# A convolution feeding a gated feed-forward layer on one core: the opening's taps, casts, bands and loads rearranged

## The chip, the core and the metric

The kernel runs on one core of a Trainium2 chip. The metric is device time in microseconds (us), the median of several runs. Engines are named as in the profile: PE is TensorE (PEld its weight loads), DVE is VectorE, ACT is ScalarE, POOL is GpSimd, SP is SyncE, which here only issues transfers. A "q" behind a name (SPq) is the engine's instruction queue.

## The reference

A causal convolution of seven taps along the sequence, with softmax-normalised taps per head, and then a feed-forward layer with the gate h * cos(h):

```python
w = exp(weight - max(weight))          # weight: 8 heads x 7 taps
w = w / (sum(w) + 1e-9)
x_pad = concatenate([zeros(B, 6, D), x], axis=1)
x_unf = x_pad[:, idx, :].reshape(B, S, 7, 8, 24)
y = einsum('hk,bskhg->bshg', w, x_unf).reshape(32768, 192)
h = y @ w_in                            # 192 -> 2048
out = (h * cos(h)) @ w_out              # 2048 -> 192
```

B is 8, S 4096, D 192; everything comes and goes in float32.

## The kernel before

**Main loop.** The 32768 tokens are 64 tiles of 512 (index t), two tiles to a unit of 1024 (index u). For each tile, PE makes eight groups h0 to h7 of the hidden layer (`mm1`, L503, into three PSUM buffers `h`), ACT takes the cosine (L510), DVE multiplies (L514), and PE forms the output in 64 steps of `mm2` (L552). The order of PE's and ACT's work is written out by hand in strings: `PE_FIRST` and `ACT_FIRST` for the first tiles, `PE_ORDER` and `ACT_ORDER` for the rest. "m12" is twelve steps of mm2, "h3" an mm1 group, "s3" its cosine and product, "w5" five zero products, "r", "d" and "c" are parts of the convolution of coming units, "K" casts, "L" loads, "X", "Y", "T" transposes and edges, "W" the cast of half of w_out; "p" marks that a tile's 64 steps are through, so that P and Q (copies of the output out of PSUM) may follow, and "q" is a check at half a tile.

**Opening.** Before the first mm1 the first half of unit 0 must be convolved on PE. The convolution is a product with a band matrix `band` (128 x 8 heads x 256, bf16), which is built from the taps:

- `w_row` (L81) brings the 8 x 7 weights into four partitions. `quarter` (L140 to L144), a 4 x 128 matrix with ones in a block of 32 columns for each row, is made on POOL by a memset and two selections. One fp32 product (L150) spreads the four rows over four blocks of 32 partitions.
- softmax: L176 to L185 on DVE, with the exponential on ACT (L179). `mask` (L158, L159 on POOL, then copied to the other three blocks at L164 by DVE and ACT) times the taps is `prod` (L401), its sum `diag` (L404).
- sixteen copies of 32 x 76 put the pieces of `diag` into `band` (L415). The string "DPDPDPDPDPDPDPAA" gives their engines in turn. Copies 0 to 3 complete heads 0 and 1, 4 to 7 heads 2 and 3, and so on.
- x of unit 0, first half, is loaded at the very start and cast to bf16 (`cast_unit`, L219) on ACT. Its other half and unit 1 are loaded behind a no-op on SP that waits for `diag`; the loads of w_out (`load_wo`, L124, four transfers) come behind a second no-op, after `conv_first`. w_in is loaded and cast by two transfers that POOL issues (`load_w`, L112).
- PE is kept busy meanwhile with products of zeros (`keep_warm`, L136): three before L150, nine after it.
- `conv_first` (L432, copied out at L438) and `turn_first` (L453, L457) make the first four blocks of transposed input `cT`; then the main loop begins. POOL casts the rest of unit 0 (L219), unit 1, and the two halves of w_out (`cast_wo`, L120), in that order of its queue.

Each engine works its own queue in order; waits between engines are set by the data that instructions share and by the no-ops named above.

Of the kernel before, what the change touches and what calls it, by code (L numbers as in the profile page):

```python
# [8 lines left out]
FP32 = mybir.dt.float32  # L9
BF16 = mybir.dt.bfloat16  # L10
AF = mybir.ActivationFunctionType
ALU = mybir.AluOpType
# [4 lines left out]
def kernel(  # L17
# [8 lines left out]
    nc = tc.nc  # L26
    B, S, D = x.shape
    H, K = weight.shape
# [3 lines left out]
    T = 512  # L32
    NT = NTOK // T
    NB = T // 128
    U = 1024
# [41 lines left out]


    HQ = H // 4
    w_row = consts.tile([4, HQ * K], FP32)  # L80
    nc.scalar.dma_start(out=w_row, in_=weight.rearrange("(q h) k -> q (h k)", q=4))  # L81

    x_tiles = {}

# [40 lines left out]

    one = consts.tile([128, 1], FP32)
    nc.vector.memset(one, 1.0)
    zero = consts.tile([128, T], BF16)  # L130
    nc.vector.memset(zero, 0.0)  # L131
# [2 lines left out]
    def keep_warm(n, bank=idle):  # L134
        for _ in range(n):
            nc.tensor.matmul(out=bank, lhsT=zero[:, 0:128], rhs=zero, start=True, stop=True)  # L136


    quarter = consts.tile([4, 128], FP32)
    nc.gpsimd.memset(quarter, 1.0)  # L140
    nc.gpsimd.affine_select(out=quarter, in_=quarter, compare_op=ALU.is_ge, fill=0.0, base=0, pattern=[[1, 128]],
                            channel_multiplier=-32)
    nc.gpsimd.affine_select(out=quarter, in_=quarter, compare_op=ALU.is_ge, fill=0.0, base=31, pattern=[[-1, 128]],
                            channel_multiplier=32)  # L144
    scrap = consts.tile([128, 1], FP32)
    nc.scalar.activation(out=scrap, in_=one, func=AF.Exp)
    keep_warm(3)
    w_all = o_pools[1].tile([128, T], FP32, name="o_ps1")
    w_bc = w_all[:, 0 : HQ * K].rearrange("p (h k) -> p h k", k=K)
    nc.tensor.matmul(out=w_all[:, 0 : HQ * K], lhsT=quarter, rhs=w_row, start=True, stop=True)  # L150
    keep_warm(9)


    xb0 = consts.tile([128, UB + 1, D], BF16, name="x_bf0")
# [22 lines left out]
    wexp = consts.tile([128, HQ, K], FP32)  # L177
    nc.vector.tensor_tensor(out=wexp, in0=w_bc, in1=wmax.to_broadcast([128, HQ, K]), op=ALU.subtract)
    nc.scalar.activation(out=wexp, in_=wexp, func=AF.Exp)  # L179
    nc.scalar.activation(out=scrap, in_=one, func=AF.Sin)  # L180
    wsum = consts.tile([128, HQ, 1], FP32)
    nc.vector.tensor_reduce(out=wsum[:, :, 0], in_=wexp, axis=mybir.AxisListType.X, op=ALU.add)
    winv = consts.tile([128, HQ, 1], FP32)
# [168 lines left out]
    def taps(u, j, half, mul):  # L352
        if u not in pa:
            pa[u] = pa_pool.tile([128, PA, WN, OR], FP32, name="pa")
        part = slice(HALF * half, HALF * (half + 1))
        mul(pa[u][:, j, part], tap_window(u, j)[:, part], tap[:, j : j + 1])  # L356

# [1 line left out]

    def conv_raw(u):  # L360

        a, p = pa.pop(u), raw_prod
        nc.gpsimd.tensor_tensor(out=p, in0=tap_window(u, PA, K),  # L363
                                in1=tap[:, PA:K].rearrange("p (j a b) -> p j a b", a=1, b=1).to_broadcast([128, K - PA, WN, OR]),
                                op=ALU.mult)
        add = nc.gpsimd.tensor_tensor
        n, done = K - PA, 0
        while done < PA:
            m = min(n, PA - done)
            add(out=p[:, 0:m], in0=p[:, 0:m], in1=a[:, done : done + m], op=ALU.add)  # L370
            done += m
        while n > 2:
            m = n // 2
            add(out=p[:, 0:m], in0=p[:, 0:m], in1=p[:, n - m : n], op=ALU.add)  # L374
            n -= m
        ro[u] = ro_pool.tile([128, WN, OR], BF16, name="ro")
        add(out=ro[u], in0=p[:, 0], in1=p[:, 1], op=ALU.add)  # L377
# [17 lines left out]
                              in_=c[:, UB].rearrange("p c (n t) -> p n c t", t=16)[:, :, :, 8 : 8 + K - 1])  # L395


    cast_unit(0, 0, NB, nc.scalar.copy)

    prod = consts.tile([128, HQ, E, K], BF16)  # L400
    nc.vector.tensor_tensor(out=prod, in0=mask.rearrange("p (o e) k -> p o e k", o=1).to_broadcast([128, HQ, E, K]),  # L401
                            in1=wn.rearrange("p h (o k) -> p h o k", o=1).to_broadcast([128, HQ, E, K]), op=ALU.mult)
    diag = consts.tile([128, HQ, E], FP32)
    summed = nc.vector.tensor_reduce(out=diag, in_=prod, axis=mybir.AxisListType.X, op=ALU.add)  # L404

    tc.add_manual_dep(nc.sync.nop().ins, summed.ins.name, sync_dep, reason="order of the transfers")
    load_unit(0, NB, UB)
    load_unit(1, 0, NB)
    load_unit(1, NB, UB)
    load_edges(1)  # L410

    three = {"D": nc.vector.tensor_copy, "A": nc.scalar.copy, "P": nc.gpsimd.tensor_copy}
    for i, k in enumerate("DPDPDPDPDPDPDPAA"):
        q, rows = divmod(i, 4)
        three[k](out=band[32 * rows : 32 * rows + 32, HQ * q : HQ * (q + 1), 32 * rows : 32 * rows + E],  # L415
                     in_=diag[32 * q : 32 * q + 32])
    cast_unit(0, NB, UB)
    nc.gpsimd.memset(pick, 0.0)
    for i in range(2):
# [157 lines left out]
    def finish(t):  # L577
        o_sb[t] = opool.tile([128, NB, D], FP32, name="o_sb")
        for si in range(2):
            for b in range(2):  # L580
# [5 lines left out]

    PE_ORDER = ['m12 h0 m4 h1 K+3 R+1 m5 h2 m7 q h3 U+0 m6 h4 m17 h5 X+1 m9 p h6 h7 O m4', 'm11 h0 m4 h1 m6 h2 m7 q x+1 h3 m5 h4 m7 c1 m8 c2 m3 h5 T+3 L+4 m9 p O h6 h7 m4']
    ACT_ORDER = ['s0 s1 a211 s2 s3 s4 a014 a114 Q s5 P s6 s7 a007', 's0 s1 s2 a102 s3 a203 s4 Q ec2 ec1 s5 P s6 s7']  # L590

    PE_FIRST = ["K1 h0a h0b W0 h1 h2 h3 r h4 w5 d11 w4 h5 d21 W1 c11 X0 m1 h6 m11 h7 L2 c21 D1",
                "m6 K2 h0 m1 L3 h1 K3 m13 q h2 m3 h3 m9 h4 m6 h5 m3 X1 c12 m11 p c22 h6 d12 h7 L4 L5 m17 c13 m4 c23 m1 d22 Y1 D2 m1",
                "h0 m2 h1 m7 q K4 h2 m11 h3 X2 O m8 h4 Y2 m13 p h5 h6 m9 h7 m7",
                "h0 m8 h1 m8 q h2 m7 h3 m7 O m1 h4 m3 d13 m4 d23 m6 h5 m4 p T4 h6 h7 m4 D3 Z0 Z1",
                'm12 h0 m4 h1 K+3 m5 h2 m7 q h3 m6 h4 m17 h5 X+1 m9 p h6 h7 O m4',
                'm11 h0 m4 h1 m6 h2 m7 q x+1 Y3 h3 m5 h4 m7 c1 m8 c2 m3 h5 T+3 L+4 m9 p O h6 h7 m4']
    ACT_FIRST = ["s0a s0b s1 s2 er s3 s4 ed11 ed21 s5 ec11 s6 ec21 s7",
                "s0 s1 s2 s3 s4 s5 ec12 ec22 Q P s6 ed12 s7 ed22 ec13 ec23",
                "s0 s1 s2 s3 Q s4 P s5 s6 s7",  # L600
                "s0 s1 s2 s3 s4 ed13 ed23 Q s5 P s6 s7"] + ACT_ORDER

    PE_LAST = "m10 h0 m3 h1 m13 h2 m2 q h3 m10 h4 m3 h5 m7 h6 m12 p h7 O m7"
    ACT_LAST = "s0 s1 s2 s3 s4 s5 s6 P A s7"

    HALVES = {"": (0, NB), "a": (0, NB // 2), "b": (NB // 2, NB), "l": (0, NB // 2), "r": (NB // 2, NB)}
# [5 lines left out]
    for t in range(NT + 1):  # L612
        u, second = divmod(t, TPU)
        cu = u + TPU
        if t >= 2 * TPU:
            if second:
                conv["c"] = conv_unit(cu, ring_banks) if cu < NU else iter(())
        pe = PE_LAST if t == NT - 1 else "m%d p" % (2 * STEPS * NT - step) if t == NT else PE_ORDER[second] if t >= len(PE_FIRST) else PE_FIRST[t]
        act = ACT_LAST if t == NT - 1 else ACT_ORDER[second] if t >= len(ACT_FIRST) else ACT_FIRST[t]
        act, h = act.split(), {}  # L620
        done = {k for k in done if k[0] in "cd" and k[2:]}
# [4 lines left out]
        def flush():  # L626
            while act:
                k = act[0]
                if k[0] == "e":
                    need = k[1:] if k[1:] in conv else k[1] + "2" + k[3:]  # L630
                else:
                    need = "p" if k in "PQA" else "h" + k[3:] if k[0] in "ab" else "h" + (k[1:2] if k[2:] in "lr" else k[1:])
                if need not in done:
                    return
                act.pop(0)
                if k in "PQA":
                    if 0 <= made < NT - 1:
                        evac(made, int(k != "P"), nc.scalar.copy if k == "A" else None)
                elif k[0] in "ab":
                    if u + 2 in rT:  # L640
                        taps(u + 2, int(k[1]), int(k[2]), nc.scalar.mul if k[0] == "a" else nc.vector.tensor_scalar_mul)
                elif k[0] == "e":
                    next(conv[part_of(k[1:])], None)
                elif k[0] == "s" and t < NT:
                    gcu(t, int(k[1]), h[k[1:2] if k[2:] in "lr" else k[1:]], *HALVES[k[2:]])
# [17 lines left out]
        for k in pe.split():  # L663
            if k[0] == "h":
                if t < NT:
                    h[k[1:]] = mm1(t, int(k[1]), *HALVES[k[2:]])
            elif k[0] in "rdc":
                next(conv[part_of(k)], None)
            elif k[0] == "m":
                for q in range(step, step + int(k[1:])):  # L670
                    mm2_step(q)
                step += int(k[1:])
            elif k[0] == "w":
                keep_warm(int(k[1:]), o_pools[0].tile([128, T], FP32, name="o_ps0"))
            elif k == "p":
                assert step % (2 * STEPS) == 0
                made = step // (2 * STEPS) - 1
            elif k == "q":
                assert step % (2 * STEPS) == STEPS
            elif k[0] == "W":  # L680
                cast_wo(int(k[1]))
            elif k == "O":
                while stored <= made and (stored, 0) in evacs and (stored, 1) in evacs:
                    store(stored)
                    stored += 1
            elif k[1:] and k[1] != "+":
                of_unit(k[0], int(k[1]))
            else:
                if u + int(k[2:]) < NU and (k[0] not in "RUx" or u + int(k[2:]) >= FIRST_RAW):
                    of_unit(k[0], u + int(k[2:]))  # L690
            done.add(k)
            flush()
            if k == "p" and made == NT - 1:
                finish(NT - 1)
        assert t == NT or not act


# [28 lines left out]
```

## Time and profile before

| | us |
|---|---|
| median of 3 runs (lowest, highest) | 705.16 (705.04, 705.51) |
| the profiled execution | 705.18 |
| its span | 703.5 |
| PE busy | 697.0 (99% of the span) |
| DVE busy | 642.4 (91%) |
| ACT busy | 644.4 (92%) |
| POOL busy | 503.7 (72%) |
| mean granted clock of PE | 0.999 |

The profile follows one execution. "Busy" is the time in which an engine has an instruction running. A timeline line gives the start from the span's begin, the length, engine, source line, operation, the tile written and the tiles read, the shapes, how many instructions were merged, and in brackets the idle time before with what ended it. The chain is followed back from the last instruction through what released each step. In a table of stretches each engine has its busy time and, in parentheses, its instruction count; the last three columns are the granted clock, the share of the DMA engines and GB/s.

### The profile page before, as it was taken

The numbers are of one execution on the slowest core, as the hardware profiler recorded it, in microseconds if no ns is written. First come the engines' busy times: TensorE is split into PE (matmuls) and PEld (weight loads), VectorE is DVE, ScalarE is ACT, GpSimd is POOL, SyncE is SP. The second block draws the span as 40 slices with busy tenths as digits, with TensorE's granted clock in tenths as the row PEclk, the third lists the DMA queues.
The fourth block names the chain that finished last, engine by engine and source line by source line (L and its number), as shares of the span: only waits on it lengthen the run. The fifth ranks groups of instructions, "written<-read, shape, count | busy, mean of one in ns | idle before, by whom it ended". The sixth has DMA issues, their size and how long they took to land.

```text
span 703.5 us, 26826 instructions
## 1 busy us (share of the span) xinstructions
PE 697.0 (99%) x11830; PEld 512.8 (73%) x11830; DVE 642.4 (91%) x598; ACT 644.4 (92%) x831; POOL 503.7 (72%) x214
## 2 busy tenths in 40 slices
PE   8999999999999999999999999999999999999997
PEld 4677777777777777777777777777777777777776
DVE  6889999999999999999999999999999999999996
ACT  7889999999999999999999999999999999999875
POOL 6524478977778877778877688877789778799400
PEclk9999999999999999999999999999999999999999
DMA  8964456667667768676656577577665576874331
GB/s 214 234 167 97 120 135 143 138 147 164 138 153 146 131 145 176 134 152 131 147 152 153 150 159 129 140 161 150 143 147 132 145 174 137 153 127 95 92 91 47
DMA packets 228292, 100.09 MB, mean 142 GB/s; under 512 B 156240, under 2 KB 227792, under 8 KB 228176
## 3 DMA queue, kind: packets, MB, share of 16 engines
q1 hardware_dynamic: 227464, 97.40, 62.7%
q8 instruction: 92, 1.51, 0.9%
q0 software_dynamic: 416, 0.79, 0.7%
q14 instruction: 24, 0.20, 0.1%
q10 hardware_dynamic: 296, 0.20, 0.1%
HBM read 31.36 MB, written 25.17 MB: 80 GB/s over the span
## 4 chain that ended last, share of the span: by engine, by line
PE 96%; DMA 1%; DVE 1%; POOL 0%; SPq 0%; ACT 0%; issue 0%; POOLq 0%
PE o_ps L552 48%; PE h L503 46%; PE h L277 2%; DMA wo_f<-in_moe_w_out_dram 1%; PE h L552 0%; SPq L124 0%; PE h L229 0%; DVE band L415 0%; POOL wo L120 0%; POOL mask L159 0%; DVE ct L438 0%; PE o_ps L432 0%; ACT mask L164 0%; DVE diag L404 0%; DVE prod L401 0%
## 5 line engine op out<-in xcount | busy, mean ns | idle before, releaser
L514 DVE TENSOR_TENSOR g<-h,cs 128x1024 bf16<-128x1024 f32 (+1 forms) x513 | 604.9, 1216 | 27.9 <-ACT cs L510 24.5
L510 ACT ACTIVATE cs<-h 128x1024 bf16<-128x1024 f32 (+1 forms) x513 | 511.0, 1021 | 44.0 <-PE h L503 30.6
L552 PEld LDWEIGHTS <-g 64*128 64x128 bf16 x8192 | 354.2, 94 | 102.2 <-issue 1.0
L552 PE MATMUL o_ps<-wo,g 64*128 64x192 bf16 x8128 | 420.6, 243 | 0.1
L503 PE MATMUL h<-cT,w 64*128 64x512 bf16 (+1 forms) x3078 | 407.0, 376 | 0.8 <-DVE g L514 0.4
L503 PEld LDWEIGHTS <-w 64*128 64x128 bf16 x3078 | 147.6, 94 | 75.0 <-issue 1.8
L211 POOL CAST xk<-x_f 128x768 bf16<-128x768 f32 (+1 forms) x56 | 76.4, 1367 | 113.9 <-DMA x_f<-in_x_dram 109.3
L363 POOL TENSOR_TENSOR raw_prod<-rT,tap 128x2784 f32<-128x2784 bf16 x28 | 135.3, 4832 | 0.2
L370 POOL TENSOR_TENSOR raw_prod<-raw_prod,pa 128x2088 f32<-128x2088 f32 x28 | 129.1, 4609 | 2.2
L356 ACT ACTIVATE pa<-rT,tap 128x348 f32<-128x348 bf16 x168 | 94.6, 580 | 0.0
L374 POOL TENSOR_TENSOR raw_prod<-raw_prod 128x1392 f32<-128x1392 f32 x28 | 87.9, 3138 | 2.2
L571 DVE COPY o_sb<-o_ps 128x384 f32<-128x384 f32 x62 | 34.6, 557 | 23.7 <-PE o_ps L552 23.5
L377 POOL TENSOR_TENSOR ro<-raw_prod 128x696 bf16<-128x696 f32 x28 | 46.5, 1660 | 2.2
L294 ACT CAST ct_buf<-h 112x480 bf16<-112x480 f32 x56 | 28.6, 562 | 4.1 <-PE h L277 0.6
L571 ACT COPY o_sb<-o_ps 128x384 f32<-128x384 f32 x64 | 30.8, 482 | 0.1
L277 PE MATMUL h<-xk,band 64*112 64x120 bf16 x448 | 21.2, 213 | 0.0
L277 PEld LDWEIGHTS <-band 64*112 64x112 bf16 x448 | 18.0, 127 | 0.0
L219 POOL CAST x_bf<-x_f 128x768 bf16<-128x768 f32 (+2 forms) x5 | 9.1, 1812 | 7.0 <-DMA x_f<-in_x_dram 6.9
L307 POOL COPY ct<-ct 128x1728 bf16<-128x1728 bf16 x3 | 4.9, 1630 | 8.9 <-ACT ct L239 8.9
L394 POOL COPY cT<-cT 128x144 bf16<-128x144 bf16 x3 | 0.9, 308 | 13.5 <-DMA cT<-ct 13.5
L136 PE MATMUL o_ps<-zero 128*128 128x512 bf16 x21 | 7.2, 492 | 1.3 <-DVE zero L131 1.3
L239 ACT CAST ct<-h 128x432 bf16<-128x432 f32 x12 | 5.9, 530 | 0.4 <-issue 0.4
(66 smaller groups left out, 52.7 us busy)
## 6 DMA issues: line engine op xcount, KB each, us to landing
out_dram<-o_sb SPq DMA_DIRECT2D x63, 384.0 KB, 3.7
x_f<-in_x_dram SPq DMA_DIRECT2D x28, 480.0 KB, 5.5
x_f<-in_x_dram SPq DMA_DIRECT2D x56, 192.0 KB, 2.7
cT<-ro SPq DMA_DIRECT2D x112, 87.0 KB, 2.3
x_f<-in_x_dram SPq DMA_DIRECT2D x4, 384.0 KB, 5.6
wo_f<-in_moe_w_out_dram SPq DMA_DIRECT2D x4, 384.0 KB, 7.9
x_f<-in_x_dram SPq DMA_DIRECT2D x2, 768.0 KB, 5.2
cT<-ct_buf SPq DMA_TRANSPOSE x56, 4.0
```

The source lines that it names most:

```text
L211: copy(out=xk[u][:, NC * n0 : NC * n1].rearrange("p (k n) m -> p k n m", k=NC), in_=x_tiles[u][:, n0:n1].rearrange("p n (m k) -> p k n m", ...
L277: return nc.tensor.matmul(out=ps[h // 4][0:OP, 0 : NPB * 4 * G].rearrange("p (m i r) -> p i m r", m=NC * NPB, i=4)[:, h % 4], lhsT=band[si ...
L356: mul(pa[u][:, j, part], tap_window(u, j)[:, part], tap[:, j : j + 1])
L363: nc.gpsimd.tensor_tensor(out=p, in0=tap_window(u, PA, K), in1=tap[:, PA:K].rearrange("p (j a b) -> p j a b", a=1, b=1).to_broadcast([128, ...
L370: add(out=p[:, 0:m], in0=p[:, 0:m], in1=a[:, done : done + m], op=ALU.add)
L374: add(out=p[:, 0:m], in0=p[:, 0:m], in1=p[:, n - m : n], op=ALU.add)
L377: add(out=ro[u], in0=p[:, 0], in1=p[:, 1], op=ALU.add)
L503: nc.tensor.matmul(out=h[:, i, n0 * 128 : n1 * 128], lhsT=w[rows, k, j, :], rhs=rhs, start=(k == 0), stop=(k == NC - 1))
L510: nc.scalar.activation(out=cs[:, :, part], in_=h[:, :, part], func=AF.Sin, bias=math.pi / 2.0, scale=1.0)
L514: nc.vector.tensor_tensor(out=g_tiles[t][:, 2 * j : 2 * j + 2, part], in0=h[:, :, part], in1=cs[:, :, part], op=ALU.mult)
L552: ms.append(nc.tensor.matmul(out=o_ps[tt, b, si], lhsT=g_tiles[tt][rows, f, s * 128 : (s + 1) * 128], rhs=wo[rows, f // 2, f % 2, :], star ...
L571: (copy or copies[b])(o_sb[t][:, 2 * b : 2 * b + 2, :].rearrange("p s d -> p (s d)"), o_ps.pop((t, b)))
```

## The change

The weights go into one partition (`w_row` 1 x 4 x 14), `one` becomes 128 x 32, and four products of a 1 x 32 row of ones with 14 weights each replace the product with `quarter`, which goes. Eleven zeros follow instead of nine. x's first cast goes to POOL (the default of `cast_unit`). The band copies are dealt out as "DAPDAPDAPDAPDADA" and come before the SP no-op, which now waits for the last of them; the loads of unit 0's rest and unit 1 follow it. Further, in the part behind the opening, "p" and "q" leave the strings, and the "m" loop itself notes when a tile's 64 steps are complete; a few assertions are added; the tokens a and b may name a unit.

```diff
-    w_row = consts.tile([4, HQ * K], FP32)
-    nc.scalar.dma_start(out=w_row, in_=weight.rearrange("(q h) k -> q (h k)", q=4))
+    w_row = consts.tile([1, 4, HQ * K], FP32)
+    nc.scalar.dma_start(out=w_row, in_=weight.rearrange("(o q h) k -> o q (h k)", o=1, q=4))
...
-    one = consts.tile([128, 1], FP32)
+    one = consts.tile([128, 32], FP32)
...
-    quarter = consts.tile([4, 128], FP32)
-    nc.gpsimd.memset(quarter, 1.0)
-    nc.gpsimd.affine_select(out=quarter, in_=quarter, compare_op=ALU.is_ge, fill=0.0, base=0, pattern=[[1, 128]],
-                            channel_multiplier=-32)
-    nc.gpsimd.affine_select(out=quarter, in_=quarter, compare_op=ALU.is_ge, fill=0.0, base=31, pattern=[[-1, 128]],
-                            channel_multiplier=32)
...
-    nc.tensor.matmul(out=w_all[:, 0 : HQ * K], lhsT=quarter, rhs=w_row, start=True, stop=True)
-    keep_warm(9)
+    for q in range(4):
+        nc.tensor.matmul(out=w_all[32 * q : 32 * q + 32, 0 : HQ * K], lhsT=one[0:1], rhs=w_row[:, q], start=True, stop=True)
+    keep_warm(11)
...
-    cast_unit(0, 0, NB, nc.scalar.copy)
+    cast_unit(0, 0, NB)
...
-    summed = nc.vector.tensor_reduce(out=diag, in_=prod, axis=mybir.AxisListType.X, op=ALU.add)
-
-    tc.add_manual_dep(nc.sync.nop().ins, summed.ins.name, sync_dep, reason="order of the transfers")
+    nc.vector.tensor_reduce(out=diag, in_=prod, axis=mybir.AxisListType.X, op=ALU.add)
+
+    three = {"D": nc.vector.tensor_copy, "A": nc.scalar.copy, "P": nc.gpsimd.tensor_copy}
+    for i, k in enumerate("DAPDAPDAPDAPDADA"):
+        q, rows = divmod(i, 4)
+        m = three[k](out=band[32 * rows : 32 * rows + 32, HQ * q : HQ * (q + 1), 32 * rows : 32 * rows + E],
+                     in_=diag[32 * q : 32 * q + 32])
+    tc.add_manual_dep(nc.sync.nop().ins, m.ins.name, sync_dep, reason="order of the transfers")
     load_unit(0, NB, UB)
     load_unit(1, 0, NB)
     load_unit(1, NB, UB)
     load_edges(1)
-
-    three = {"D": nc.vector.tensor_copy, "A": nc.scalar.copy, "P": nc.gpsimd.tensor_copy}
-    for i, k in enumerate("DPDPDPDPDPDPDPAA"):
...
             elif k[0] == "m":
-                for q in range(step, step + int(k[1:])):
-                    mm2_step(q)
-                step += int(k[1:])
+                for _ in range(int(k[1:])):
+                    mm2_step(step)
+                    step += 1
+                    if step % (2 * STEPS) == 0:
+                        made = step // (2 * STEPS) - 1
+                        done.add("p")
+                        flush()
+                        if made == NT - 1:
+                            finish(NT - 1)
...
-            elif k == "p":
-                assert step % (2 * STEPS) == 0
-                made = step // (2 * STEPS) - 1
-            elif k == "q":
-                assert step % (2 * STEPS) == STEPS
```

## The prediction

> **What bounds the kernel.** I read the page's chain first, then the waits from 20 us to the end, then the first 24 us in order of time.
>
> ```profile
> span 703.5 us, 26826 instructions
> ...
> PE 96%; DMA 1%; DVE 1%; POOL 0%; SPq 0%; ACT 0%; issue 0%; POOLq 0%
> ```
>
> The chain in order of time (start, length) has, after 8.84 us of a w_out transfer:
>
> ```profile
> 21.00 0.02 issue
> 21.02 0.02 POOLq L120
> 21.04 0.08 issue
> 21.12 1.48 POOL wo L120
> 22.60 0.04 issue
> 22.64 0.34 PE o_ps L552 x4
> ```
>
> From 22.64 to 699.9 us TensorE never lets go of the chain: 677 us of its own work, which this diff leaves alone, and behind it only the last copy and store. What the change is worth is how far it moves that 22.64, so the opening is the only stage to cost. The page's 91 to 92% for VectorE and ScalarE play no part.
>
> Two roads lead to 22.64. Road A is computation: the softmax taps become the band, the first convolution runs, the first mm1 starts. Road B is transfers: w_out lands at 21.00 and is cast by L120.
>
> ```profile
> 2.06 0.96 POOL L159 TENSOR_SCALAR_AFFINE_SELECT mask<-mask 32x266 bf16<-32x266 bf16 x1
> 2.70 0.60 PE L150 MATMUL o_ps<-w_row,quarter 4*128 4x14 f32 x2
> 2.98 1.43 POOL L112 DMA_DIRECT2D w<-in_moe_w_in_dram  x2
> 3.55 0.17 DVE L178 TENSOR_TENSOR wexp<-o_ps,wmax 128x14 f32<-128x14 f32 x1
> 3.91 0.21 ACT L179 ACTIVATE wexp<-wexp 128x14 f32<-128x14 f32 x1
> 5.28 0.71 DVE L404 TENSOR_REDUCE diag<-prod 128x76 f32<-128x532 bf16 x1
> 6.02 1.86 DVE L415 CAST band<-diag 32x76 bf16<-32x76 f32 x7
> 6.13 2.00 POOL L415 CAST band<-diag 32x76 bf16<-32x76 f32 x7 [0.73 <-DVE diag L404]
> 10.60 1.62 PE L503 MATMUL h<-cT,w 64*128 64x256 bf16 x18 [0.18 <-DVE cT L457]
> 11.73 1.23 POOL L219 CAST x_bf<-x_f 128x768 bf16<-128x768 f32 x1 [3.59 <-DMA x_f<-in_x_dram]
> 22.05 0.93 PE L552 MATMUL o_ps<-wo,g 64*128 64x192 bf16 x12
> ```
>
> In this timeline the bands are the last thing before the convolution: GpSimd's seventh ends at 8.13, 2.14 after diag (5.99). Road A has a slack of about 0.27 at the end: of the twelve matmuls at 22.05, eight need only w_out's first half and at the usual 40 ns each are through near 22.37; the other four wait for 22.64.
>
> **The change, part by part.** Road A first.
>
> Taps. One fp32 product has two passes, 0.24 us apart (0.60 in all less 0.38, the longest one's length, rounded up). Four products make eight passes. No row shows a 128x32 fp32 weight. From above: the same 0.24 per pass; the taps then end 6 x 0.24 = 1.4 later. From below: L337's two small bf16 products (0.20 us in all, each some 0.17) are 0.03 apart, so eight passes end about as early as now. I take 0.10, nearer the low end since only a quarter of the columns is loaded: 7 x 0.10 less 0.24 = +0.46. Of this 0.16 is hidden: the exponential started at 3.91 although its input was ready at 3.72, because ScalarE was still copying the mask (L164, to 3.88). That copy comes earlier, since GpSimd loses the three quarter instructions (0.19 + 0.28 + 0.28 and their gaps, 0.85) and the mask is ready at 2.2. So diag: +0.30 (bounds -0.15 to +1.3). The Trainium skill, "TensorE: Matmul & The Clock Gate", section "LDWEIGHTS (loading the stationary operand)", makes the load's time proportional to columns; that would be an estimated 0.06 per pass and diag at about 0.0 instead of +0.30. No row here tests it.
>
> Bands. Sixteen copies go from 7 D, 7 P, 2 A to 6 D, 6 A, 4 P. At their rows: D 6 x 0.27 = 1.60; A 6 x 0.255 = 1.53; P 4 x 0.29 = 1.14. The longest, 1.60, replaces 2.14: -0.54. ScalarE is free in time: exponential, 1.28 of table load, 0.20, all before diag ends, as it no longer casts x.
>
> x cast by GpSimd. 1.23 for the same shape (11.73 row) instead of 1.21 on ScalarE. Behind two w issues, two memsets and ident, which end at 5.40 now and 4.55 then, it ends at 5.8, before diag at 6.3: costed at nothing. The first x load lands 3.4 after its issue at 0.82, so it doesn't wait. The cover is 0.5; beyond that every 0.1 delays the four P copies, which have another 0.46 before they are last. The row speaks of a cast beside a VectorE that reads PSUM; VectorE's band copies take 0.19 alone and 0.25 to 0.29 beside GpSimd's, so a mutual slowing of a third is the upper end: 6.2, still covered. The Trainium skill, "GPSIMD Engine Reference", section "Specifications", says that GpSimd shares its SBUF interface with VectorE when that has two SBUF inputs; by it prod (L401, 0.48) would stretch, at most by a third, and road A lose 0.15.
>
> Eleven zeros. The early ones are 0.43 apart, later ones 0.22; the step came at about 5.9.
>
> ```profile
> 5.34 0.15 PEld L136 LDWEIGHTS <-zero 128*128 128x128 bf16 x1 [0.28 <-issue]
> ...
> 5.77 0.15 PEld L136 LDWEIGHTS <-zero 128*128 128x128 bf16 x1 [0.28 <-issue]
> ...
> 6.12 0.10 PEld L136 LDWEIGHTS <-zero 128*128 128x128 bf16 x1 [0.20 <-issue]
> ```
>
> Starting at 3.6, six at 0.43 reach 6.1 and five at 0.22 then 7.2. The last band comes at 5.99 + 0.30 + 1.60 = 7.9, and twelve of the convolution's first matmuls (25 ns each, L432) fit between: nothing. If all took 0.43 they would end at 8.3 (a rival below).
>
> The ones tile grows from 128x1 to 128x32: VectorE's memset of 0.06 stays under 0.1, ahead of a TensorE that waits for the next memset: 0.03 at most. The weight vector in one partition: the load was through well before 2.70, when TensorE's three zeros ended; nothing.
>
> Road A: +0.30 - 0.54 = **-0.24** at the first mm1 (10.60). Its w must be there: the second w load, issued at 3.78, landed 6.6 later at 10.4; its issue moves by -0.85, so 9.5.
>
> Road B. The nop on SyncE now waits for the last band (7.9) instead of diag (6.0). Behind it on SP: four x issues (0.39, 0.50, 0.69, 0.79), a nop, four w_out issues, then all later transfers. GpSimd waits for the first of them (11.73 row). The price depends on the time from issue to landing, of which the x tile's view (to 12 us) gives both ends; the second fence is the view of stretches of 1 us.
>
> ```profile
> DMA to landing us min/median/max: 3.4/5.6/6.4
> ```
>
> ```profile
> 6.00:7.00 1.00, 0.85 (x7) 0.26 (x5) 0.92 (x4) 0.98 (x2) 0.73 (x4) 1.00 1.04 158
> ...
> 10.00:11.00 1.00, 0.82 (x13) 0.50 (x12) 0.99 (x2) 0.69 (x2) 0.00 (x0) 1.00 1.09 369
> ```
>
> 3.4 is the opening load, alone; 5.6 is unit 0's rest, issued at 6.01 while w filled the engines (in the stretch from 6 to 7 us the last two columns, DMA share and GB/s, read 1.04 and 158). Now w is through at 9.5, and an issue at 7.9 with the 3.4 lands at 11.3 instead of 11.7: **-0.4**. With the 5.6 it is 13.5: +1.8. I take 3.4, because 5.6 holds the wait behind w, which moves forward. The stretch from 9 to 18 us runs at 318 GB/s without a gap, so all that follows in this queue, w_out too, moves by the same -0.4. The w_out issues come 0.5 later (10.4 instead of 9.9), hidden behind the x data until about 14. GpSimd's casts of units 0 and 1 and the convolution behind them move with the data.
>
> Later parts. The strings lose "p" and "q", and the m loop marks a finished tile itself. Each p stood right behind the m that completed 64 steps, so I read the same instructions in the same order: 0, from 22.64 to the end.
>
> Sum: road A arrives at 22.37 - 0.24 = 22.13, road B at 22.64 - 0.4 = 22.24. The later one counts: -0.4. The profiled execution took 705.18 (span 703.5 and 1.7 around it), 0.02 from the median 705.16, so **704.8**, own range 704.3 to 705.4.
>
> **Rivals.** Differences within 0.2% (1.41 us; 703.75 to 706.57) are about what a measurement of this kernel can't tell from no change.
>
> *The held load is simply late* (slower). The time from issue to landing stays near 5.6, because the four x issues meet their own queue and w's tail. For: the median and the longest x landing of that view are 5.6 and 6.4. Against: both stood behind w. Unit 0's rest lands at 13.5, w_out at 22.8, the cast ends at 24.4: +1.8, 707.0 (706.2 to 707.3). It decides as soon as that load lands after 11.7, and GpSimd's idle time before its second x cast would show it.
>
> *The taps cost the full row.* 0.24 a pass: diag +1.26, road A +0.72, the nop opens at 5.99 + 1.26 + 1.60 = 8.85, x lands at 12.25 (+0.6). Road B is the later one: +0.6, 705.8. For: the only fp32 row. Against: a quarter of the columns.
>
> *TensorE steps up late.* The small products break up the activity behind the step at 5.9. Eleven zeros at 0.43 end at 8.3, the 32 matmuls of L432 at 50 ns instead of 25 take 1.6, so 9.9 instead of 8.9, with the 12 transposes another 0.3: road A +1.3 less the slack 0.27, 706.2; a longer spell costs more. Against: nine zeros and a pair of fp32 products have been enough. The Trainium skill, "TensorE: Matmul & The Clock Gate", section "The HAM clock gate", has a free-running window of about 3.4 us behind the step; zeros from 1.31 and a step at 5.9 agree with it, but which part of a window the taps fall into isn't known before.
>
> *Both roads gain more* (faster). From 19 to 21 us the DMA moved 30 and 60 GB/s while w_out had not landed: a straggling tail of some 2 us. If it vanishes in the new order, road B is off the path, and road A decides: with the taps at their low end -0.15 - 0.54, then the slack's 0.27, then 0.45 if the waits on the way shrink (0.15 at 21.41 for g, 0.3 where the first d11 stands behind unit 1's cast at 16.6). That is -1.4: 703.8 (703.2 to 704.4). Against: every one of these must hold.
>
> **Chances.** Forecast 0.40; held load 0.20, three quarters of it over 706.57; taps 0.10 (0.02 over); late step 0.10 (half over); both gain 0.20, half of it below 703.75. So faster 0.10, slower 0.15 + 0.02 + 0.05 = 0.22, the same 0.68. The range 703.6 to 706.9 leaves out about a tenth at each end.
>
> **What would show it.** Taps: the span of the small products near 2.7 (0.7 plus one length, as against 0.6 now) and the exponential near 4.2. Bands: six VectorE copies within 1.6 of diag. GpSimd's first x cast over by 6.0. The second x cast starting near 11.3 and not 13. The wo cast of the second half ending before 22.3. First mm1 at about 10.4. I am wrong if the x data starts later than 9.5, if zeros are still 0.43 apart after 7, or if any wait shows on TensorE after 23 us.

## The result: 0.2% slower, and the profile after

The changed kernel takes 706.64 us in the median, against 705.10 for the kernel before beside it (16 runs each, all sessions together; 705.88 to 708.72 and 705.01 to 705.51). The ratio is 1.0023, with an interval of 1.0016 to 1.0030. The sign of the forecast was wrong. The profiled execution took 706.42, 1.24 more than the one of before.

Head and chain shares of the page after:

```profile
span 704.7 us, 26835 instructions
...
PE 97%; ACT 1%; DMA 1%; DVE 1%; POOL 0%; issue 0%; ACTq 0%; POOLq 0%
```

As before, TensorE holds the end. It goes from tile 1's first mm1 group to its last instruction in 677.19 us (677.10 before), so the rewritten m loop is worth 0.09. That first group starts at 23.86 instead of 22.81: 1.05 of the 1.24 lies ahead of it. The tail has 0.04 and the time outside the span 0.06.

The opening's timeline (start, length, engine, line, operation, tiles, shapes):

```profile
2.06 1.43 POOL L112 DMA_DIRECT2D w<-in_moe_w_in_dram  x2
2.63 0.30 PE L145 MATMUL o_ps<-w_row,one 1*32 1x14 f32 x8
2.83 0.83 ACT L159 COPY mask<-mask 32x266 bf16<-32x266 bf16 x2
3.69 0.21 ACT L174 ACTIVATE wexp<-wexp 128x14 f32<-128x14 f32 x1
4.25 1.20 POOL L214 CAST x_bf<-x_f 128x768 bf16<-128x768 f32 x1
4.34 1.14 DVE L180 TENSOR_TENSOR wn<-wexp,winv 128x14 bf16<-128x14 f32 x1
6.03 0.71 DVE L401 TENSOR_REDUCE diag<-prod 128x76 f32<-128x532 bf16 x1
6.77 1.61 ACT L406 CAST band<-diag 32x76 bf16<-32x76 f32 x6 [1.35 <-DVE diag L401]
10.85 1.62 PE L499 MATMUL h<-cT,w 64*128 64x256 bf16 x18 [0.18 <-DVE cT L453]
13.41 1.22 POOL L214 CAST x_bf<-x_f 128x768 bf16<-128x768 f32 x1 [5.42 <-DMA x_f<-in_x_dram]
18.14 0.53 PE L224 MATMUL h<-x_bf,band 128*128 128x216 bf16 x4 [0.69 <-POOL x_bf L214]
```

The taps are quicker: the exponential starts 0.22 earlier. Then one line stands out. `wn`, VectorE's product of 14 numbers, takes 1.14 and ends at 5.48, as GpSimd's cast ends at 5.45. Before, it took 0.17:

```profile
4.56 0.17 DVE L185 TENSOR_TENSOR wn<-wexp,winv 128x14 bf16<-128x14 f32 x1
```

So `diag` is done at 6.74 instead of 5.99 and the last band copy at 8.38 instead of 8.13, and only then does the no-op let the loads of x go. GpSimd waits for them until 13.41 instead of 11.73. The chain in order of time (start, length, what) passes from compute to the held transfer and back through GpSimd's casts:

```profile
8.13 0.26 ACT band L406
8.40 4.89 DMA x_f<-in_x_dram
...
15.48 1.06 POOL x_bf L214
16.62 1.49 POOL x_bf L214
18.14 0.53 PE h L224 x4
...
21.44 1.24 DVE g L510
22.72 0.82 PE h L499 x6
```

The transfer lies between 8.40 and 13.29. Before, it was issued at 6.01 and landed at 11.61, 5.6 later. Now it needs 4.9, but from an issue 2.4 later. The chain no longer passes through w_out, whose second half is cast by 22.53 (22.60 before). The lateness comes through GpSimd's casts instead: the convolution's four matmuls at 18.14 came at 16.62 before, and of the 1.68 at the landing 1.05 are left at tile 1's first mm1.

What stood in the DMA engines' way is seen in the stretch from 9 to 10 us (the last three columns are the clock, the DMA share and GB/s); before:

```profile
9.00:10.00 1.00, 0.94 (x11) 0.48 (x10) 0.96 (x2) 0.57 (x2) 0.00 (x0) 1.00 1.08 242
```

and after:

```profile
9.00:10.00 1.00, 0.89 (x13) 0.44 (x9) 0.85 (x1) 0.57 (x2) 0.00 (x0) 1.00 0.63 51
10.00:11.00 1.00, 0.82 (x13) 0.52 (x12) 0.95 (x3) 0.91 (x2) 0.00 (x0) 1.00 0.69 204
```

Before, x's rest had stood in the queues behind w_in and came as w_in thinned out. After, it was asked for only at 8.40, and while w_in thinned out little came: 51 GB/s, a gap in the transfers. The first packet of x's rest is hardly later (9.46 against 9.34), but by its 256th the load is 0.62 behind (10.89 against 10.27). Then 15 of the 16 DMA engines are through at 12.43, and the last one at 13.29; before, these were 11.59 and 11.61.

### The profile page after: what moved, and what is told of

Its sections match the earlier page's. It is cut to its first block, busy times and chain, and to the rows that moved or that the text cites. A ratio compares the mean times of both kernels' runs of the same rounds, so it can differ in the third digit from the quotient of the medians.

```text
span 704.7 us, 26835 instructions
## 1 busy us (share of the span) xinstructions
PE 697.0 (99%) x11836; PEld 520.6 (74%) x11838; DVE 643.3 (91%) x597; ACT 644.0 (91%) x834; POOL 503.0 (71%) x209
## 4 chain that ended last, share of the span: by engine, by line
PE 97%; ACT 1%; DMA 1%; DVE 1%; POOL 0%; issue 0%; ACTq 0%; POOLq 0%
PE o_ps L548 47%; PE h L499 47%; PE h L272 2%; DMA x_f<-in_x_dram 1%; PE h L548 0%; POOL x_bf L214 0%; PE h L224 0%; ACT band L406 0%; ACT L140 0%; DVE g L510 0%; DVE wn L180 0%; ACT cs L506 0%; PE o_ps L136 0%; ACT mask L159 0%; DVE diag L401 0%
## 5 line engine op out<-in xcount | busy, mean ns | idle before, releaser
L548 PEld LDWEIGHTS <-g 64*128 64x128 bf16 x8192 | 359.1, 94 | 97.4 <-issue 0.7
L499 PEld LDWEIGHTS <-w 64*128 64x128 bf16 x3078 | 153.1, 94 | 71.6 <-issue 1.8
```

The lines of the kernel that those rows point to most:

```text
L499: nc.tensor.matmul(out=h[:, i, n0 * 128 : n1 * 128], lhsT=w[rows, k, j, :], rhs=rhs, start=(k == 0), stop=(k == NC - 1))
L548: ms.append(nc.tensor.matmul(out=o_ps[tt, b, si], lhsT=g_tiles[tt][rows, f, s * 128 : (s + 1) * 128], rhs=wo[rows, f // 2, f % 2, :], star ...
```

## The experiments

Three suspects came out of this reading: the **port** (the x cast on GpSimd stops `wn`), the **hold** (the no-op waits for the last band), and, later, **early w** (`load_w` issued at 2.06 instead of 2.98, because `quarter` went). Each experiment has eleven executions beside the kernel before (medians 705.07 to 705.14), except c1, which has one. With an interval of some ±0.6 us for each ratio, a difference of 0.7 between two kernels is at the edge of what one pair can show. The spans of the same executions scatter less (703.4 in the median for the kernel before, 704.7 for the changed one), so they are given where they decide. They differ by 1.3 and the times by 1.54: some 0.2 of the loss lies outside the span. It shows only in kernels with the four small products (b1 and b3 have it, b2 doesn't), and its cause stays open.

### Undoing the hold, the cast, or the wait

**The no-op back on `diag`** (e1), the rest as changed:

```diff
-    nc.vector.tensor_reduce(out=diag, in_=prod, axis=mybir.AxisListType.X, op=ALU.add)
+    summed = nc.vector.tensor_reduce(out=diag, in_=prod, axis=mybir.AxisListType.X, op=ALU.add)
+    tc.add_manual_dep(nc.sync.nop().ins, summed.ins.name, sync_dep, reason="order of the transfers")
+    load_unit(0, NB, UB)
...
-    tc.add_manual_dep(nc.sync.nop().ins, m.ins.name, sync_dep, reason="order of the transfers")
-    load_unit(0, NB, UB)
...
```

> The changed kernel with one part undone: the no-op on SyncE waits for diag again, and the x loads come ahead of the band copies. Theory H (the hold): what costs is that the x loads are issued late, so that unit 0's rest lands at 13.3 instead of 11.6 and GpSimd's casts, the first d11 and all behind it are late. Then the issue comes at about 6.8, the load lands near 11.3, the second x cast starts by 11.6, the first d11 by 16.8, and the time is 705.2 (704.9 to 705.5), although wn still takes 1.1. Theory P (the shared port): what costs is that VectorE's wn (0.17 before, 1.14 now) waits out GpSimd's x cast, so that diag, the bands and the first mm1 are late. Then the time stays at 706.3 to 706.7.

Measured: 705.82, ratio 1.0011 (1.0002 to 1.0020). The no-op opens at 6.8 and x lands at 11.86. The time lies between the ranges of both theories: neither the hold nor the port is the whole loss. Opening the no-op earlier is worth 0.8 of the 1.5, and 0.7 stays.

**The x cast back on ScalarE** (e2):

```diff
-    cast_unit(0, 0, NB)
+    cast_unit(0, 0, NB, nc.scalar.copy)
```

> The changed kernel with x's first cast back on ScalarE, all else as changed. Theory P: wn takes 0.17 again, diag ends at 5.8 instead of 6.74; the band copies on ScalarE wait for its cast until 6.6 and end near 8.2; time 705.3 to 705.8. Theory H: the no-op still opens only with the last band, at about 8.2 instead of 8.4, so the time moves by no more than 0.3: 706.3 to 706.6.

Measured: 706.66, ratio 1.0025 (1.0016 to 1.0034): no gain. `wn` is back at 0.17, but ScalarE casts until 6.53 and only then starts its six band copies, which end at 8.16. The no-op opens at 8.18, hardly earlier. This is what the expectation had for theory H (an opening near 8.2, 706.3 to 706.6), but for 0.06; theory P's 705.3 to 705.8 missed. With `wn` quick and the no-op late, the whole loss stays.

**The x cast stays on GpSimd, but waits for `prod`** (e3):

```diff
-    cast_unit(0, 0, NB)
-
...
-    nc.vector.tensor_tensor(out=prod, in0=mask.rearrange("p (o e) k -> p o e k", o=1).to_broadcast([128, HQ, E, K]),
+    made_prod = nc.vector.tensor_tensor(out=prod, in0=mask.rearrange("p (o e) k -> p o e k", o=1).to_broadcast([128, HQ, E, K]),
...
+    def cast_held(out, in_):
+        m = nc.gpsimd.tensor_copy(out=out, in_=in_)
+        tc.add_manual_dep(m.ins, made_prod.ins.name, sync_dep, reason="cast behind prod")
+
+    cast_unit(0, 0, NB, cast_held)
```

> The changed kernel with GpSimd's first x cast made to wait for prod, so that it no longer runs beside wn or prod. Both theories: wn 0.17, diag at about 5.8, the bands end at 7.4 to 7.8. Theory P: all of the loss goes, 705.0 or less. Theory H: the no-op opens near 7.6, the load lands at about 12.5 against 11.6 in the kernel before, and half the loss stays: 705.7 to 706.1. If wn still took over 0.5, the cast would not be its cause.

Measured: 705.80, ratio 1.0010 (1.0002 to 1.0019). Its timeline:

```profile
4.34 0.17 DVE L180 TENSOR_TENSOR wn<-wexp,winv 128x14 bf16<-128x14 f32 x1
...
5.06 0.71 DVE L405 TENSOR_REDUCE diag<-prod 128x76 f32<-128x532 bf16 x1
5.09 1.21 POOL L400 CAST x_bf<-x_f 128x768 bf16<-128x768 f32 x1 [0.83 <-DVE prod L396]
...
5.80 0.55 DVE L410 CAST band<-diag 32x76 bf16<-32x76 f32 x1
```

Two readings. `wn` has its 0.17 again, so the cast was what stopped it, while the reduction, which reads one SBUF tensor, runs beside the same cast at its usual 0.71. One input is not enough to be spared, though: VectorE's first band copy came while the cast ran and took 0.55 instead of 0.19, ending 0.05 after it. And with the hold still in place, but opening at 7.43, x lands at 12.09 and the loss is again 0.7: theory H's range, while P's 705.0 missed.

**Both, no-op on `diag` and cast behind `prod`** (e4), with the two diffs above:

> Both edits together: the no-op on diag and GpSimd's cast behind prod. Diag at 5.8, x issued at 5.8, landing at 11.0 to 11.4, first mm1 near 10.2 (w is through by about 10.3 at the latest). Both theories: at or under the kernel before, 704.4 to 705.1. If it stays above 705.5, a third part of the change costs.

Measured: 705.88, ratio 1.0011 (1.0003 to 1.0020). Both theories had 704.4 to 705.1, and both missed. Each repair alone takes away as much as both together, and 0.8 of the loss is neither of them. The trace shows a new wait: TensorE's first mm1 group stands 1.04 for w_in.

```profile
11.47 1.47 PE L503 MATMUL h<-cT,w 64*128 64x256 bf16 x17 [1.04 <-DMA w<-in_moe_w_in_dram]
```

**The cast in four pieces** (c1, a single execution), to see what `wn` waits for: if the port is lent for a whole instruction, `wn` should end with the first piece.

```diff
-    cast_unit(0, 0, NB)
+    def cast_pieces(out, in_):
+        for i in range(4):
+            nc.gpsimd.tensor_copy(out=out[:, 8 * i : 8 * i + 8], in_=in_[:, 8 * i : 8 * i + 8])
+
+    cast_unit(0, 0, NB, cast_pieces)
```

> A look only: the changed kernel with GpSimd's first x cast in four pieces of about 0.35. If VectorE's two-input wn has to wait for the GpSimd instruction that is running, it gets in between two pieces: wn at 0.5 or less, diag about 0.7 earlier. If it shares the port for as long as GpSimd has work, wn stays over 1.

```profile
4.28 0.43 POOL L397 CAST x_bf<-x_f 128x192 bf16<-128x192 f32 x1
4.34 0.41 DVE L180 TENSOR_TENSOR wn<-wexp,winv 128x14 bf16<-128x14 f32 x1
```

`wn` ends 0.04 after the piece that ran when it came. It waits out one instruction; it is not slowed in proportion. `prod`, also with two SBUF inputs, then takes 0.65 beside the pieces instead of 0.48. The one time, 706.38, decides nothing.

### The remainder: w_in's earlier load

The kernels so far issue GpSimd's first load while the opening load of x is still under way. w_in's second half then landed at 10.83 in e1, 11.11 in e2 and 11.43 in e4, against 10.42 before (at 10.30 and 10.27, though, in the changed kernel and e3). Moving `load_w` behind `ident` brings its first issue from 2.06 to 2.77 (2.98 before):

```diff
-    for t in range(2):
-        load_w(t)
...
+    for t in range(2):
+        load_w(t)
```

**With cast and no-op as in e4 too** (w1):

> e4_held_diag with one more edit: the two w_in transfers are issued behind ident's selection, near 2.9 us, where the kernel before issued them (2.98), instead of at 2.06. Theory W: what e4 still lost is that an earlier w_in meets the tail of x's opening load; its packets get up to 0.9 us long, the 16 DMA engines drift apart, the last one ends w_in as late as before or later (11.4 in e4, 10.4 before), and every transfer that needs all engines waits for the last. Then w_in lands by 10.5, unit 0's rest by 11.6, the time is 704.5 to 705.1, and the runs lie within 0.7 of each other as those of the kernel before do. Rival Z: the loss comes from eleven zeros, the band order or the cast's place, and the time stays at 705.6 to 706.0.

Measured: 705.13, ratio 1.0002 (0.9993 to 1.0011), span 703.2 against 704.1 in e4. The zeros, the band order and the new loop are still in this kernel, so the remainder was none of them. **With the late load alone** (w2):

> The changed kernel with only that edit: w_in issued near 2.9. Theory W: the late-engine share goes, the shared port and the hold stay: 705.6 to 706.1, in a narrower spread. GpSimd's x cast may now start behind the issue of w_in, near 4.3 as in the changed kernel, so wn stays near 1.1. Rival Z: no change, 706.4 to 706.8.

Measured: 706.51, ratio 1.0017 (1.0009 to 1.0026). That is the rival's number; theory W's 705.6 to 706.1 missed. The same edit is worth 0.75 where the others are undone, and 0.1 where they stand. **With the port conflict alone left** (w3: late load, no-op on `diag`):

> The changed kernel with the no-op back on diag and w_in issued late; of the three costs only the shared port is left (wn 1.1, diag at 6.7, x issued at 6.8). If port and hold cost only together (the load is issued behind the end of w_in, near 10): unit 0's rest still queues behind w_in, lands by 11.8, and the time is 705.0 to 705.4. If the port costs by itself through the late first mm1 (10.8 instead of 10.5): 705.5 to 705.9.

Measured: 705.55, ratio 1.0006 (0.9997 to 1.0015); x lands at 11.61. The time lies in the second range, but the span is 703.5, so only 0.1 is lost inside it.

From the other side, **the kernel before with the four products and no `quarter`** (b1), which pulls `load_w` to 2.06:

```diff
-    w_row = consts.tile([4, HQ * K], FP32)
...
+    w_row = consts.tile([1, 4, HQ * K], FP32)
...
-    nc.tensor.matmul(out=w_all[:, 0 : HQ * K], lhsT=quarter, rhs=w_row, start=True, stop=True)
+    for q in range(4):
+        nc.tensor.matmul(out=w_all[32 * q : 32 * q + 32, 0 : HQ * K], lhsT=one[0:1], rhs=w_row[:, q], start=True, stop=True)
```

> The kernel before with one part of the change alone: the taps by four small products, without quarter. GpSimd reaches the w_in transfers at 2.06. Theory W: w_in meets x's tail here too: slower, 705.5 to 706.0, runs over 1 us apart, some engine ending w_in after 10.2. Rival Z: diag comes 0.2 earlier and nothing else moves: 704.8 to 705.1.

Measured: 705.95, ratio 1.0011 (1.0002 to 1.0020), span 703.9. **The same with the late load** (b3):

> b1_taps (the kernel before with the four small products) with w_in issued behind ident, near 2.8 instead of 2.06. Theory W: the 0.8 that b1 lost came from the early w_in alone, so it goes: w_in lands by 10.5, unit 0's rest by 11.7, time 704.8 to 705.2. If the four products or the one-partition weights cost by themselves, it stays near 705.9.

Measured: 705.10, ratio 1.0002 (0.9994 to 1.0011), span 703.2. The view of tile w gives the issue and the time to landing; first with the early load, then with the late one:

```profile
L112 POOL DMA_DIRECT2D w<-in_moe_w_in_dram x2: 630/717/804, 2.1 to 2.9; - x2
...
DMA to landing us min/median/max: 7.5/8.3/9.0
```

```profile
L112 POOL DMA_DIRECT2D w<-in_moe_w_in_dram x2: 630/717/804, 2.8 to 3.6; - x2
...
DMA to landing us min/median/max: 5.7/6.3/6.9
```

Issued 0.7 earlier, the second half lands 1.4 later (2.86 + 9.0 = 11.9 against 3.6 + 6.9 = 10.5). That is the worst case: b1's profile fell on its longest span, and in all traces of kernels with the whole opening load the early issue (2.06) landed between 10.27 and 11.85, an issue at 2.77 or later between 10.27 and 10.53. In b1, TensorE's first mm1 waits for it; waits of the early-load kernel from 9 to 13 us (total, times, longest):

```profile
PE h L498 <- DMA w<-in_moe_w_in_dram: 1.3, 1, 1.3
```

**Is it the meeting with x's opening load?** These two kernels, b1 and b3 otherwise, load only the first two of the opening's four blocks and cast them twice, so part of the first tile's output differs; w is early in the first (x1), late in the second (x2; moved as above):

```diff
-    load_unit(0, 0, NB)
+    load_unit(0, 0, NB // 2)
...
-    cast_unit(0, 0, NB, nc.scalar.copy)
+    bf[0] = xb0
+    for s in range(2):
+        nc.scalar.copy(out=xb0[:, 1 + 2 * s : 3 + 2 * s, :].rearrange("p n (h k r) -> p (n h) k r", k=NC, r=R),
+                       in_=x_tiles[0][:, 0:2, :].rearrange("p n (h r k) -> p (n h) k r", k=NC, r=R))
```

> b1_taps (w_in issued at 2.06) with x's opening load cut to its first two blocks of four; the cast reads these two twice, so a part of the first tile's output is another. The opening load is through by about 3.2 and w_in's data, from 3.65, no longer meet it. Theory W (the collision with x's tail): the early w_in costs nothing now; w_in lands 5.5 to 6.9 after its issues as in the kernel before (7.5 to 9.0 in b1), the last by 9.9, and the time is 704.8 to 705.2. Rival E (early as such: SyncE's or GpSimd's other work, or the order of issue at 2.06): landing stays over 7, time 705.6 to 706.0.

> The control of x1_half_early: the same half load and cast, with w_in issued late as in b3_taps_late_w (2.77). Both theories: 704.9 to 705.2; the difference of x1 to this one is what the early w_in costs without a collision: under 0.2 by theory W, 0.6 to 0.9 by rival E.

Measured: 704.81, ratio 0.9999 (0.9990 to 1.0008), and 705.00, 0.9999 (0.9990 to 1.0008); the spans are 703.0 and 703.1, against 703.9 in b1. With x's load out of the way, the early w lands in an ordinary time:

```profile
L112 POOL DMA_DIRECT2D w<-in_moe_w_in_dram x2: 630/717/804, 2.1 to 2.9; - x2
...
DMA to landing us min/median/max: 5.7/6.3/7.0
```

The stretch from 3 to 4 us shows the difference, first with the whole x load (DMA share 1.21), then with half (0.29):

```profile
3.00:4.00 1.00, 1.00 (x3) 0.30 (x2) 0.41 (x3) 0.95 (x4) 0.93 (x4) 1.00 1.21 222
```

```profile
3.00:4.00 1.00, 1.00 (x3) 0.30 (x2) 0.42 (x3) 0.95 (x4) 0.93 (x4) 1.00 0.29 33
```

**An issue in between** (x3), at 2.25 (one memset moved ahead of it):

> b1_taps with w_in issued behind one memset of GpSimd, near 2.35, between the early (2.06) and the late (2.77) one; its data start near 3.95, when all but the last few of x's packets are through. Theory W: most of the cost goes, 705.1 to 705.5, landing 5.7 to 7.2. Rival E: in proportion, about 705.6 or more.

Measured: 705.55, ratio 1.0007 (0.9998 to 1.0016); w needs 6.3 to 8.1. Both lie between what theory W (705.1 to 705.5, up to 7.2) and rival E (705.6 or more) had, so this run doesn't decide between them.

### The hold by itself, and a try at a gain

**The kernel before with its no-op on the last band copy** (b2):

```diff
-    tc.add_manual_dep(nc.sync.nop().ins, summed.ins.name, sync_dep, reason="order of the transfers")
...
-        three[k](out=band[32 * rows : 32 * rows + 32, HQ * q : HQ * (q + 1), 32 * rows : 32 * rows + E],
+        m = three[k](out=band[32 * rows : 32 * rows + 32, HQ * q : HQ * (q + 1), 32 * rows : 32 * rows + E],
...
+    tc.add_manual_dep(nc.sync.nop().ins, m.ins.name, sync_dep, reason="order of the transfers")
```

> The kernel before with the hold alone: the no-op on the last band copy in the list (ScalarE's, 7.30 in the kernel before) instead of diag (5.99). Theory H: unit 0's rest is issued 1.3 later, and since w_in still fills the engines until 10.0, lands 0.3 to 0.8 later; the second x cast near 12.3, the time 705.4 to 706.0. If the hold costs nothing while w_in runs: 705.0 to 705.2. If it costs its full 1.3: 706.4.

Measured: 705.16, ratio 1.0000 (0.9991 to 1.0009). The no-op opens at 7.31, 1.3 later than before, and x lands at 11.68, 0.07 later. (The no-op waits for the last copy in the list, ScalarE's; GpSimd's last band copy ends later, at 8.13.) From 9 to 10 us the engines are as full as before:

```profile
9.00:10.00 1.00, 0.89 (x10) 0.49 (x10) 0.96 (x2) 0.57 (x2) 0.00 (x0) 1.00 1.05 267
```

In w2, whose no-op opens at 8.39, they are not, and x lands at 13.21:

```profile
9.00:10.00 1.00, 0.89 (x12) 0.42 (x9) 0.87 (x1) 0.57 (x2) 0.00 (x0) 1.00 0.59 100
```

Last, **`pick` (a mask that GpSimd makes) before GpSimd's second x cast**, in w1 (f1), since GpSimd waits there anyway:

```diff
-    cast_unit(0, NB, UB)
     nc.gpsimd.memset(pick, 0.0)
...
+    cast_unit(0, NB, UB)
```

> w1_late_w_clean with pick made ahead of GpSimd's second x cast, where GpSimd stands idle, instead of behind it. If the road is x's landing, GpSimd's three casts and the first d11, then unit 1's first cast starts 0.7 earlier (13.1), its second when the edges have landed (14.8), d11 about 0.25 earlier (16.3), and the time falls by 0.2 to 0.4: 704.7 to 705.0. If w_out decides: unchanged, 705.1.

Measured: 705.21, ratio 1.0002 (0.9993 to 1.0011): no gain. w_out's first half landed only at 18.5 in its profile, so the time saved on GpSimd met another wait.

All eight combinations of the three suspects, times in us and median spans in parentheses (703.4 for the kernel before; early w: `load_w` at 2.06, else 2.77 to 2.98):

| | neither | port | hold | port and hold |
|---|---|---|---|---|
| late w | 705.13 (703.2), 705.10 (703.2) | 705.55 (703.5) | 705.16 (703.5) | 706.51 (704.5) |
| early w | 705.88 (704.1), 705.95 (703.9) | 705.82 (703.9) | 705.80 (703.8) | 706.64 (704.7) |

The second figures under "neither" (b3, b1) and the hold with late w (b2) start from the kernel before, the others from the changed one. e2 is not in the table: early w and no port, but a no-op that opens at 8.18, and with 706.66 (704.8) it is as slow as the last column. So what the last column shows is a late opening, not the port as such: where the no-op opened by 7.43 the spans are 703.2 to 704.1, where it opened at 8.18 or later 704.5 to 704.8 (c1's single execution, 7.84 and 704.6, lies with these).

No version beat the kernel before by more than its interval.

## Why the prediction was wrong, step by step

**The hold, -0.4 (road B): the step that failed.** "[A]n issue at 7.9 with the 3.4 lands at 11.3 instead of 11.7". It opened at 8.40 and needed 4.9. The reading behind it, that the 5.6 held a wait behind w, was right (b2: an issue 1.3 later lands 0.07 later). The conclusion was not: a wait that has gone can only be taken out down to what the load costs by itself, and that price in this place had been read from the only other load, at the very start. With w late, an issue at 7.31 was free, and one at 8.39 landed at 13.21. No such load behind `diag` took less than 4.36 in any trace (e2, issued at 8.18), so even the forecast's 7.9 would have landed near 12.3 (an estimate from these). The path was wrong too. The forecast led x's landing to the end through w_out; w_out's cast ended no later than before, and the loss came through GpSimd's casts of x.

**The x cast on GpSimd, "costed at nothing": the second failure.** I asked whether the cast ends before `diag`; I should have asked whom it stops while it runs. The product named was `prod`, stretched "at most by a third" (0.15). It was `wn`, and it was blocked outright: 0.97. That made `diag` late by 0.75, and with it the last band, so that the no-op opened at 8.40 and not at 7.9. By the Trainium skill, "SBUF — State Buffer", section "SBUF: two separate sides", a VectorE instruction with two SBUF inputs and a GpSimd instruction that reads SBUF take a lock for the whole instruction, and the second fully blocks. The trace agrees: 1.14 beside a cast of 1.20, 0.41 beside pieces of 0.43.

**The second w load at 9.5: third failure.** "Its issue moves by -0.85, so 9.5" kept the 6.6 to landing. In the changed kernel it took 7.4 and landed at 10.30, and in b1 9.0. Road A's first mm1 came at 10.85, so there w was in time by 0.5; with the other two undone w was itself the wait (1.04 at the first mm1 in e4, 1.25 in b1), and against the same kernels with w late (w1, b3) the loss was 0.75 and 0.85 in the time, 0.9 and 0.7 in the span. In the changed kernel this cost is nearly hidden behind the hold (0.1).

**What held.** Bands: the last ends 1.64 after `diag` instead of 2.14, -0.50 against -0.54, although ScalarE's six copies were the longest (1.61) and not VectorE's (1.49). Eleven zeros: done by 6.77, the step in their spacing at 5.74, nothing lost. The m loop: 0.09 in 677. The taps had the wrong sign: not +0.30 but -0.22 at the exponential, of which 0.07 is this trace's earlier origin, since eight passes take 0.30 in all. The -0.15 that is left is the forecast's lower bound. More wasn't to be had: the exponential's input was ready at 3.38, and ScalarE was still copying the mask until 3.66. These copies started at 2.83, behind ScalarE's table load and a first short activation, and not when the mask was ready (2.09), as the forecast had it. Where the taps stand alone (b3), the end hardly moves: 705.10 against 705.11, and a span of 703.2 against 703.4.

**The rivals.** The held load being simply late was nearest: 707.0 against 706.64, decided, as it said, by a landing after 11.7 and shown by GpSimd's idle time. Its price was near partly by luck: the issue came 0.5 later than it had and the load took 4.9 and not 5.6, and its way to the end, a w_out cast that ends at 24.4, did not occur. The forecast's sign that x's data start later than 9.5 did not come either (9.46), and yet the load was late. The taps' full row and a late step did not occur, nor did a gain on both roads.

**Open.** Why x's rest needs 4.9 into nearly empty queues where the opening load needs 3.4 was not tried. The trace splits the lateness in two, a slow start (0.62 at the 256th packet) and one engine that ends 0.86 behind the others; neither has a shown cause. That an issue is free as long as the queues are full is read from b2 and w2, not tested by itself. That the collision works through the engines drifting apart is not shown: in b1 they end w_in's second half 2.9 apart, in b3 0.7, but single long packets occur with late w too (up to 1.56 in w1). That early w adds its cost rests on two pairs and on x1, in times each near the size of an interval, in spans 0.7 to 0.9.

## What to carry to other kernels

Costs in this opening didn't add: a later issue was free while the queues held another load (up to about 7.3 here) and cost about 1 us from 8.2 on, and a delay elsewhere can carry it over that edge. Before moving a cast to GpSimd, list VectorE's instructions with two SBUF inputs, and its copies from SBUF to SBUF, in the time it runs, small ones first. And a deleted instruction moves everything behind it on its engine; ask which transfer now starts earlier and which one it meets.

## What the hardware showed

- A 14-element product waited for the end of GpSimd's running cast (0.17 to 1.14); a one-input reduction beside the same cast kept its 0.71, but a one-input copy went from 0.19 to 0.55 (e3).
- Eight fp32 passes of 1 x 32 weights into four column blocks took 0.30 in all, where the former single product of two passes took 0.60; within each group of four the starts lie 7 ns apart, and 55 ns lie between the groups. The Trainium skill, "TensorE: Matmul & The Clock Gate", section "Part 3: Packing small matmuls — row/col tiling", gives about 4 ns of issue overhead for each further tile; the 7 ns here are of the same order.
- A casting load issued 0.7 earlier, into the tail of another load, landed between 0.2 earlier and 1.4 later than the same load issued late (10.27 to 11.85 against 10.45 in b3); with that other load halved it landed at 9.86 (x1).
